# Batch 2's x groups one and a half units apart in a fused attention and bilinear-FFN kernel, and the loads of batches 4 to 7 issued one output later

## The chip, the cores and the metric

The kernel runs on one core of a Trainium2 chip. The metric is device time in microseconds (us) of one execution. The profile names the engines PE (TensorE matmul), PEld (TensorE weight load, which overlaps PE), DVE (VectorE), ACT (ScalarE), POOL (GpSimd) and SP (SyncE, here only a DMA issuer; its sequencer is SPq). L258 means line 258 of the kernel.

## The reference, cut to what matters

```python
# q, k, v: (8 batches, 8 heads, 576 tokens, 64)      w_a, w_b: (512, 1536)    w_out: (1536, 512)
kv  = einsum('bhsd,bhse->bhde', k, v)
out = einsum('bhsd,bhde->bhse', q, kv)                 # "x" before its normalization
x   = out / sqrt(mean(out**2, -1) + 1e-6) * g_norm     # heads joined: (4608 tokens, 512)
y   = ((x @ w_a) * (x @ w_b)) @ w_out                  # (4608, 512)
```

The FFN is most of the arithmetic. The attention is linear: one 64x64 matrix kv for each head, then q times kv, then a normalization over each head's 64 values.

## The kernel before

The 4608 tokens are cut into nine strips of 512. In strip s (counted from 0), PE makes 12 *units* (each 4 matmuls with w_a, then 4 with w_b, then ACT copies a out of PSUM and DVE multiplies b by it), and after them 4 *outputs* (12 matmuls with w_out each). In the strips 1 to 6 the attention of batch s+1 is made between those matmuls. Its places are counted in units and outputs: place 9 is behind unit 9, place 9.5 in the middle of unit 10, place 12 behind the first output, 15 behind the last.

A batch has 576 tokens, so five *chunks*: four of 128 tokens and one of 64. Each chunk passes through five steps on four engines.

```python
def tx(self, c, i):                       # x group of chunk c, into PSUM bank i
    t0 = c * 128
    n = min(128, S - t0)
    for p in range(NP):                   # 4 matmuls, 128 columns each
        nc.tensor.matmul(P[0:n, i, p * 128 : (p + 1) * 128],
                         lhsT=self.qT[:, p, t0 : t0 + n], rhs=kvb[self.b % 2][:, p, :],
                         start=True, stop=True)
    nc.scalar.activation(sqt[c % 3][0:n], P[0:n, i, :]..., AF.Square)
# tss(c): DVE sums the squares by head.   trs(c): ACT takes the reciprocal root, POOL multiplies
#         it by g into sqt[c % 3].
def txt(self, c, i):                      # the last reader of bank i
    nc.vector.tensor_mul(t[0:n], P[0:n, i, :]..., sqt[c % 3][0:n])
    nc.sync.dma_start_transpose(xt[:, :, t0 : t0 + n], ...)      # x, transposed, for the FFN
# ... cut ...
def slot(A, s, n):
    k0, xs = (5, (6.5, 7.5, 8.5, 9.5, 10.5)) if s == 1 else (2, (3.5, 5, 6, 7.5, 8.5))
    # ... the kv products at place k0: cut ...
    for c, x in enumerate(xs):
        i = 5 + c % 3                     # banks 5, 6, 7, then 5 and 6 again
        if n == x:          A.tx(c, i)
        elif n == x + 0.5:  A.tss(c)
        elif n == x + 1:    A.trs(c)
        elif n == x + 2.5:  A.txt(c, i)

for s in range(1, N_STRIP - 1):
    b = s + 1
    for n in range(FC + 4):               # 12 units, then 4 outputs
        # ... unit or output n, with slot(A, s, n - 0.5) in its middle: cut ...
        slot(A, s, n)
        if s == 1 and n == 3:
            load_late(3)
        if b + 1 < B and n == (12 if s == 1 else 8):
            transpose_q(b + 1)            # a DMA transpose on SP
        if b + 2 < B and n == 13:
            load_late(b + 2)              # POOL: waits for that transpose, then issues six DMAs
```

In these traces each engine works off its own instructions in the order in which the program names them; "The spacing alone" below shows what this costs when one of them waits (DVE stood for 9.77 us, at the end with two products ready behind it). Strip 1 starts its x groups later than the other strips (6.5 instead of 3.5), because batch 2's q, k and v are still on their way.

Of the kernel before, what the change touches and what calls it, by code (L numbers as in the profile page):

```python
# [15 lines left out]
def kernel(  # L16
# [13 lines left out]
    B, H, S, D = q.shape  # L30
# [102 lines left out]
    def load_late(b):  # L133
        if b > EARLY:

            nc.gpsimd.tensor_copy(gate, qT[(b - 1) % 2][0:1, 0, 0:1])
        d = qs_d[b].rearrange("t (h d) -> t h d", h=H)
        for hs in (slice(0, NP), slice(NP, H)):
            nc.gpsimd.dma_start(out=d[:, hs, :], in_=q[b, hs].rearrange("h t d -> t h d"))  # L139
        n = 128 * LC  # L140
        for t, src in ((ktl[b % 2], k), (vtl[b % 2], v)):
            nc.gpsimd.dma_start(
                out=t[:, :, 0:LC, :],
                in_=src[b, :, 0:n].rearrange("h (t c) d -> t h c d", c=LC),
            )
            nc.gpsimd.dma_start(
                out=t[0 : S - n, :, LC, :], in_=src[b, :, n:].rearrange("h t d -> t h d")
            )

    def transpose_q(b):  # L150
        nc.sync.dma_start_transpose(qT[b % 2], qs_d[b])
# [149 lines left out]
    class Unit:  # L301
        n = 0
# [36 lines left out]
    def ab_bank():  # L339
        n_ab[0] += 1  # L340
        return AB[(n_ab[0] - 1) % len(AB)]

    def ffn_ab(s, fc, between=None):
        u = Unit(s, fc, ab_bank(), ab_bank())
        u.part_a()
        if between:
            between()
        u.part_b()
# [38 lines left out]
    def ffn_o(s, g, i=O, between=None):  # L387
        o_mm(s, g, i, range(FC // 2))
        if between:
            between()  # L390
        o_mm(s, g, i, range(FC // 2, FC))
        o_out(s, g, i)
# [154 lines left out]
    def slot(A, s, n):  # L547

        kb = P[:, 7, 0 : NP * D].rearrange("q (p e) -> q p e", e=D)
        k0, xs = (5, (6.5, 7.5, 8.5, 9.5, 10.5)) if s == 1 else (2, (3.5, 5, 6, 7.5, 8.5))  # L550
        if n == k0:
            for p in range(NP):
                A.kv(p, kb[:, p, :])
            A.kv_out(slice(0, NP), kb)
        for c, x in enumerate(xs):
            i = 5 + c % 3
            if n == x:
                A.tx(c, i)
            elif n == x + 0.5:
                A.tss(c)  # L560
            elif n == x + 1:
                A.trs(c)
            elif n == x + 2.5:
                A.txt(c, i)

    for s in range(1, N_STRIP - 1):
        b = s + 1
        A = Attn(b) if b < B else None
        for n in range(FC + 4):
            amid = (lambda n=n: slot(A, s, n - 0.5)) if A else None  # L570
            if n >= FC:
                ffn_o(s, n - FC, ab_bank() if n % 2 else O, amid)
            elif s > 1 or n > 1:
                ffn_ab(s, n, amid)
            if A:
                slot(A, s, n)

            if s == 1 and n == 3:
                load_late(3)
            if b + 1 < B and n == (12 if s == 1 else 8):  # L580
                transpose_q(b + 1)
            if b + 2 < B and n == 13:
                load_late(b + 2)
    last = N_STRIP - 1
    for fc in range(FC):
# [41 lines left out]
```

## Time and profile before

| | before |
|---|---|
| median time, first 3 runs | 318.99 us |
| span in the profile | 317.4 us |
| PE busy | 310.9 us (98%) |
| strip 1, from its first unit to strip 2's | 34.65 us |
| each of strips 2 to 6 | 33.27 or 33.28 us |

PE is the engine that bounds the kernel. These are lines of the page of the kernel before: the span, and busy time, share of the span and number of instructions by engine.

```profile
span 317.4 us, 4979 instructions
...
PE 310.9 (98%) x1907; PEld 147.6 (46%) x1907; DVE 138.2 (44%) x230; ACT 115.8 (37%) x229; POOL 101.8 (32%) x124
```

A 98% busy PE hides what is lost, so the reading goes by stretches. This is the table of stretches of the kernel before, cut where the strips 1, 2 and 3 begin: start and end, length, then busy time of each engine, granted clock (PEclk, the share of its full clock that PE was given), DMA share and GB/s; the last two are not used here.

```profile
core 0: us, PE busy (x) PEld busy (x) DVE busy (x) ACT busy (x) POOL busy (x), PEclk, DMA share, GB/s
50.77:85.42 34.65, 33.48 (x205) 15.85 (x204) 16.46 (x26) 13.05 (x27) 11.76 (x12) 1.00 1.26 169
85.42:118.69 33.27, 33.27 (x205) 15.76 (x204) 15.71 (x24) 12.75 (x26) 18.49 (x19) 1.00 1.22 145
118.69:151.97 33.28, 33.28 (x206) 15.79 (x204) 15.70 (x24) 12.75 (x26) 11.86 (x12) 1.00 0.88 122
```

Strip 1 does the same matmuls in 1.37 us more. The list of PE's waits in the kernel before says where: who waited for whom, in total, how often, and the longest.

```profile
PE P L258 <- DVE qv L292: 1.2, 2, 0.6
```

The timeline of the kernel before shows the two places. First PE: start, length, what, and in brackets the idle time before it and what ended that. Between its x groups PE makes half a unit in 0.86 us (the printed 1.03 us contains the end of the last matmul, which overlaps the next).

```profile
68.53 1.03 PE L312 MATMUL P<-xt,wb_t 128*128 128x512 bf16 x4
69.40 1.03 PE L312 MATMUL P<-xt,wa_t 128*128 128x512 bf16 x4
71.01 0.38 PE L258 MATMUL P<-kvb,qT 128*128 128x128 bf16 x4 [0.58 <-DVE qv L292]
71.23 1.03 PE L312 MATMUL P<-xt,wb_t 128*128 128x512 bf16 x4
72.09 1.03 PE L312 MATMUL P<-xt,wa_t 128*128 128x512 bf16 x4
73.70 0.38 PE L258 MATMUL P<-kvb,qT 128*64 128x128 bf16 x4 [0.58 <-DVE qv L292]
```

Then DVE in the same kernel and stretch:

```profile
69.67 0.69 DVE L330 TENSOR_TENSOR ab<-P,asb 128x512 bf16<-128x512 f32 x1 [0.67 <-PE P L312]
70.28 0.68 DVE L292 TENSOR_TENSOR qv<-P,sqt 128x512 bf16<-128x512 f32 x1
```

The x group of chunk 3 is due at 69.40 + 0.86 = 70.26. Its bank, 5, still holds chunk 0. The last reader of chunk 0 is the DVE multiply L292, which stands behind unit 9's own product L330 and ends at 70.96. PE starts at 71.01, 0.75 us late; of this the profile shows 0.58 as idle, because it draws the last matmul to its modelled end. Chunk 4 repeats it one unit later. The Trainium skill ("Perfetto Trace Analysis", Optimization Strategy) says that the same gap repeating on the engine that should be saturated can mean that there is not enough SBUF or PSUM for the next tile; two equal gaps of 0.58 us before the only two x groups that reuse a bank are such a case.

### The profile page before, as it was taken

The numbers are of one execution on the slowest core, as the hardware profiler recorded it, in microseconds if no ns is written. First come the engines' busy times: TensorE is split into PE (matmuls) and PEld (weight loads), VectorE is DVE, ScalarE is ACT, GpSimd is POOL, SyncE is SP. The second block draws the span as 40 slices with busy tenths as digits, with TensorE's granted clock in tenths as the row PEclk, the third lists the DMA queues.
The fourth block names the chain that finished last, engine by engine and source line by source line (L and its number), as shares of the span: only waits on it lengthen the run. The fifth ranks groups of instructions, "written<-read, shape, count | busy, mean of one in ns | idle before, by whom it ended". The sixth has DMA issues, their size and how long they took to land.

```text
span 317.4 us, 4979 instructions
## 1 busy us (share of the span) xinstructions
PE 310.9 (98%) x1907; PEld 147.6 (46%) x1907; DVE 138.2 (44%) x230; ACT 115.8 (37%) x229; POOL 101.8 (32%) x124
## 2 busy tenths in 40 slices
PE   8999999999999999999999999999999999999995
PEld 3444454444445444544454445444544444444443
DVE  5543345367137613771258225741485144213421
ACT  3733155453246314640355025512461233123310
POOL 8944890193163550347023801310042000000000
PEclk9999999999999999999999999999999999999999
DMA  8999999999799799069916992363012300020002
GB/s 179 196 196 199 200 182 150 228 125 159 167 166 140 128 155 208 4 130 136 228 13 123 124 221 38 69 115 99 2 34 57 116 4 0 33 93 8 0 33 101
DMA packets 94237, 36.19 MB, mean 114 GB/s; under 512 B 64902, under 2 KB 89734, under 8 KB 94214
## 3 DMA queue, kind: packets, MB, share of 16 engines
q0 software_dynamic: 59120, 18.44, 53.4%
q1 hardware_dynamic: 34738, 17.01, 22.9%
q10 hardware_dynamic: 356, 0.43, 0.5%
q8 instruction: 15, 0.25, 0.3%
q14 instruction: 8, 0.07, 0.1%
HBM read 37.78 MB, written 12.98 MB: 160 GB/s over the span
## 4 chain that ended last, share of the span: by engine, by line
PE 85%; DMA 7%; POOL 4%; issue 1%; DVE 1%; ACT 0%; POOLq 0%; DVEq 0%
PE P L312 52%; PE P L369 28%; DMA wb_t<-in_moe_w_b_dram 6%; PE P L258 2%; PE P L168 2%; DMA vt<-in_v_dram 2%; POOL qt L116 1%; POOL wo_t L131 1%; POOL kt L116 1%; POOL vt L116 1%; POOL wa_t L427 0%; POOL wb_t L427 0%; DVE qv L292 0%; PE P L192 0%; PE P L219 0%
## 5 line engine op out<-in xcount | busy, mean ns | idle before, releaser
L330 DVE TENSOR_TENSOR ab<-P,asb 128x512 bf16<-128x512 f32 x108 | 74.5, 691 | 111.3 <-PE P L312 93.8
L312 PE MATMUL P<-xt,wa_t 128*128 128x512 bf16 x432 | 111.9, 379 | 0.0
L312 PE MATMUL P<-xt,wb_t 128*128 128x512 bf16 x432 | 111.7, 379 | 0.1
L326 ACT CAST asb<-P 128x512 bf16<-128x512 f32 x108 | 63.1, 586 | 91.2 <-PE P L312 91.2
L369 PE MATMUL P<-wo_t,ab 128*128 128x512 bf16 (+1 forms) x444 | 95.6, 373 | 0.0
L369 PEld LDWEIGHTS <-ab 128*128 128x128 bf16 x444 | 43.1, 98 | 49.1
L312 PEld LDWEIGHTS <-wa_t 128*128 128x128 bf16 x432 | 41.3, 98 | 47.1 <-issue 0.2
L312 PEld LDWEIGHTS <-wb_t 128*128 128x128 bf16 x432 | 41.2, 98 | 47.2 <-DMA wb_t<-in_moe_w_b_dram 0.6
L282 POOL TENSOR_TENSOR sqt<-rst,g_all 128x512 f32<-128x512 f32 (+1 forms) x24 | 25.0, 1044 | 97.4 <-ACT rst L275 97.4
L382 ACT COPY osb<-P 128x512 f32<-128x512 f32 x17 | 10.0, 586 | 74.2 <-PE P L369 59.6
L384 DVE COPY osb<-P 128x512 f32<-128x512 f32 x18 | 12.4, 691 | 47.2 <-PE P L369 42.6
L139 POOL DMA_DIRECT2D qs<-in_q_dram x12 | 19.8, 1655 | 1.2 <-issue 0.9
L271 DVE TENSOR_REDUCE sst<-sqt 128x8 f32<-128x512 f32 (+1 forms) x24 | 16.2, 676 | 0.8 <-ACT sqt L265 0.8
L292 DVE TENSOR_TENSOR qv<-P,sqt 128x512 bf16<-128x512 f32 (+1 forms) x24 | 16.2, 678 | 0.0
L265 ACT ACTIVATE sqt<-P 128x512 f32<-128x512 f32 (+1 forms) x24 | 14.2, 593 | 1.6 <-PE P L258 1.6
L258 PEld LDWEIGHTS <-qT 128*128 128x128 bf16 (+1 forms) x120 | 8.9, 100 | 9.5 <-issue 4.0
L258 PE MATMUL P<-kvb,qT 128*128 128x128 bf16 (+1 forms) x120 | 11.7, 220 | 1.2 <-DVE qv L292 1.2
L275 ACT ACTIVATE rst<-sst,eps_t 128x8 f32<-128x8 f32 (+1 forms) x30 | 9.0, 301 | 4.3 <-DVE sst L271 4.3
L179 ACT CAST kvb<-P 64x256 bf16<-64x256 f32 (+1 forms) x20 | 6.0, 301 | 11.3 <-PE P L168 11.2
L233 DVE SCALAR_TENSOR_TENSOR xt<-P,g_col,rs 128x288 bf16<-128x288 f32 x16 | 7.5, 512 | 5.2 <-ACT rs L223 5.2
L131 POOL DMA_DIRECT2D wo_t<-in_moe_w_out_dram x12 | 6.4, 533 | 6.7 <-DMA wb_t<-in_moe_w_b_dram 3.2
L282 POOL TENSOR_TENSOR k_x<-rst,g_all 128x512 f32<-128x512 f32 x6 | 6.3, 1044 | 7.0 <-ACT rst L275 7.0
(66 smaller groups left out, 120.4 us busy)
## 6 DMA issues: line engine op xcount, KB each, us to landing
out_dram<-osb SPq DMA_DIRECT2D x23, 256.0 KB, 2.4
qs<-in_q_dram POOLq DMA_DIRECT2D x12, 288.0 KB, 6.9
ktl<-in_k_dram POOLq DMA_DIRECT2D x6, 512.0 KB, 10.1
vtl<-in_v_dram POOLq DMA_DIRECT2D x6, 512.0 KB, 12.5
out_dram<-osb SPq DMA_DIRECT2D x13, 128.0 KB, 2.3
wo_t<-in_moe_w_out_dram POOLq DMA_DIRECT2D x12, 128.0 KB, 5.9
wa_t<-in_moe_w_a_dram POOLq DMA_DIRECT2D x5, 256.0 KB, 9.3
wb_t<-in_moe_w_b_dram POOLq DMA_DIRECT2D x5, 256.0 KB, 9.9
```

The lines of the kernel that those rows point to most:

```text
L139: nc.gpsimd.dma_start(out=d[:, hs, :], in_=q[b, hs].rearrange("h t d -> t h d"))
L258: nc.tensor.matmul(P[0:n, i, p * 128 : (p + 1) * 128], lhsT=self.qT[:, p, t0 : t0 + n], rhs=kvb[self.b % 2][:, p, :], start=True, stop=True,)
L265: nc.scalar.activation(sqt[c % 3][0:n], P[0:n, i, :].rearrange("t (h d) -> t h d", h=H), AF.Square)
L271: nc.vector.reduce_sum(sst[c % 3][0:n], sqt[c % 3][0:n], axis=mybir.AxisListType.X)
L282: nc.gpsimd.tensor_mul(sqt[c % 3][0:n], rst[c % 3][0:n].unsqueeze(2).to_broadcast([n, H, D]), g_all[0:n].unsqueeze(1).to_broadcast([n, H, D]),
L292: nc.vector.tensor_mul(t[0:n], P[0:n, i, :].rearrange("t (h d) -> t h d", h=H), sqt[c % 3][0:n])
L312: nc.tensor.matmul(self.a if w is wa_t else self.b, lhsT=w[:, kc, self.fc * 128 : (self.fc + 1) * 128], rhs=xt[:, kc, t0 : t0 + STRIP], st ...
L326: nc.scalar.copy(self.t, self.a)
L330: nc.vector.tensor_mul(abt[self.s % 2][self.fc], self.b, self.t)
L369: nc.tensor.matmul(P[:, i, e0:e1], lhsT=abt[s % 2][fc][:, g * 128 : (g + 1) * 128], rhs=wo_t[:, fc, e0:e1], start=(fc == 0), stop=(fc == F ...
L382: nc.scalar.copy(t, P[:, i, :])
L384: nc.vector.tensor_copy(t, P[:, i, :])
```

## The change

The intent is to keep the reuse of a bank away from its last reader, by spreading batch 2's x groups. Their steps then reach into the outputs, so the load that follows on POOL is moved behind the last of them.

```diff
-        k0, xs = (5, (6.5, 7.5, 8.5, 9.5, 10.5)) if s == 1 else (2, (3.5, 5, 6, 7.5, 8.5))
+        k0, xs = (5, (6.5, 8, 9.5, 11, 12.5)) if s == 1 else (2, (3.5, 5, 6, 7.5, 8.5))
...
-            if b + 2 < B and n == 13:
+            if b + 2 < B and n == 14:
                 load_late(b + 2)
```

Chunk 3 now comes at place 11, two units after chunk 0's multiply at place 9; before it was half a unit (9.5 against 9). The second edit holds for the loads of batches 4 to 7 alike. No operation is added or taken away.

## The prediction

> **What bounds the kernel now.** TensorE. The page gives PE 310.9 us busy of a 317.4 us span (98%), granted clock 0.999; the chain that ended last is 85% PE. The Trainium skill ("Trainium Kernel Development and Optimization", Performance Expectations) warns that matmul busy time is a poor measure because matmuls are pipelined, so I read stretches and idle times instead. The table of stretches, cut where each strip's first unit begins, gives 33.27 or 33.28 us for each of strips 2 to 6, and 34.65 us for strip 1 (50.77 to 85.42), with the same 204 to 206 matmuls. Strip 1, which holds batch 2's x, is 1.37 us too long. PE's waits name the cause: "P L258 <- DVE qv L292", 2 times, 1.2 us. In the timeline the fourth x group starts at 71.01 instead of 70.26 and the fifth at 73.70 instead of 72.95.
>
> **Why it waits.** Chunks rotate over PSUM banks 5, 6, 7. Chunk 3 reuses chunk 0's bank at place 9.5, half a unit (0.86 us of PE) after chunk 0's last reader, the DVE multiply, is issued at place 9. The multiply stands behind the unit's own product on DVE: product 69.67 to 70.28, multiply 70.28 to 70.96, so PE restarts at 71.01. Chunk 4 on chunk 1's bank repeats this. In later strips the same reuse is 1.5 units apart and no wait shows.
>
> **What the change does.** No work is added or removed. x groups go to 6.5, 8, 9.5, 11, 12.5. Chunk 3 now comes 2 units (3.4 us) after chunk 0's multiply is issued; product and multiply need 1.3 us. Chunk 4 likewise. Both waits should vanish whole. The last x group moves into the output groups (halves of 1.29 us of PE), where ACT and DVE idle 3 to 5 us before each eviction, so nothing should queue.
>
> The load of batch 4: GpSimd's built order is unchanged. At place 13 the load would stand in front of chunk 4's GpSimd multiply, now at 13.5; place 14 keeps it behind. Its first instruction waits for the transpose of batch 3's q (landed 85.62), not for the place, so it starts within 2 us of before. In later strips place 14 should do nothing.
>
> **The new risk.** Chunk 2's multiply is issued at place 12 instead of 11, behind the first output eviction; its DMA transpose moves behind that eviction's stores, from 76.48 to an estimated 78.1 us. Transposes here landed 3.5 to 7.2 us after issue, the slow ones while batch 3's load (last landing 78.2) was moving. I estimate a landing at 81.5 to 83; strip 2's first product needs it at about 84.2. Slack is 1 to 2.7 us: most likely nothing is lost.
>
> **Sum.** 1.37 us saved, all on the critical path, as PE runs without a gap from there to the last output. 318.99 - 1.37 = 317.6 us, 0.4% faster. Range 317.2 to 318.5. Chances: faster by over 2% 0.01, within 2% 0.98, slower 0.01.
>
> **What would show it.** Right: PE's wait for DVE qv is gone; strip 1's stretch is 33.3 us; PE busy is unchanged; strip 2 starts near 84.1. Wrong: PE idle at strip 2's first unit, released by a DMA of xt; or output matmuls waiting for DVE or ACT copies at 76 to 84 us; or batch 3's first GpSimd multiply (96.94) delayed by the load, and PE waiting in strip 2.
>
> **What would make it wrong.** Chunk 2's transpose landing over 6 us after its issue, slowed by the stores or q's transpose, eats the gain.

## The result, and the profile after

| | before | after |
|---|---|---|
| median, 6 runs each | 319.09 us (318.94 to 319.32) | 317.71 us (317.46 to 317.88) |
| span in the profile | 317.4 us | 316.0 us |
| PE busy | 310.9 us | 309.6 us |
| strip 1 | 34.65 us | 33.28 us |

The ratio is 0.9955, with a 95% interval of 0.9943 to 0.9968. A ratio here is the mean time of one kernel's fast runs over that of the other's fast runs of the same rounds, so it is not quite the ratio of the medians.

From the page of the changed kernel:

```profile
span 316.0 us, 4979 instructions
...
PE 309.6 (98%) x1907; PEld 147.0 (47%) x1907; DVE 138.5 (44%) x230; ACT 115.9 (37%) x229; POOL 101.7 (32%) x124
```

PE's busy time is 1.3 us less although its matmuls are the same. Only 0.20 us of this is in strip 1 (33.48 and 33.28 in the tables of stretches). By the same tables 1.05 us lies before strip 1 (48.83 and 47.78), in a stretch that is equally long in both kernels, so it has nothing to do with the gain.

The table of stretches of the changed kernel, cut at the same places of the program:

```profile
50.74:84.02 33.28, 33.28 (x206) 15.76 (x204) 16.65 (x26) 13.18 (x27) 11.93 (x13) 1.00 1.33 174
84.02:117.30 33.28, 33.28 (x206) 15.78 (x204) 15.70 (x24) 12.74 (x26) 18.31 (x18) 1.00 1.32 145
```

Strip 1 is now as long as every other; the strips 2 to 6 stay at 33.27 or 33.28 us, so the load's move does nothing in them. The list of PE's waits no longer has L258; all that it has is in the first 14 us. The timeline of PE in the changed kernel around the same two x groups:

```profile
71.97 1.03 PE L312 MATMUL P<-xt,wb_t 128*128 128x512 bf16 x4
72.83 0.39 PE L258 MATMUL P<-kvb,qT 128*128 128x128 bf16 x4
73.05 4.05 PE L369 MATMUL P<-wo_t,ab 128*128 128x512 bf16 x18
77.03 0.41 PE L258 MATMUL P<-kvb,qT 128*64 128x128 bf16 x4
77.37 6.65 PE L369 MATMUL P<-wo_t,ab 128*128 128x512 bf16 x30
83.86 1.03 PE L312 MATMUL P<-xt,wa_t 128*128 128x512 bf16 x4
```

There is no bracket with an idle time, at the x groups or at strip 2's first unit. Chunk 0's multiply ran on DVE from 70.03 to 70.71, two microseconds before chunk 3 wanted its bank at 72.83.

What the change postponed can be seen on SP. This is the timeline of SP in the changed kernel:

```profile
76.56 1.12 SPq L362 DMA_DIRECT2D out_dram<-osb  x2
77.77 1.24 SPq L296 DMA_TRANSPOSE xt<-qv  x1
79.18 2.38 SPq L151 DMA_TRANSPOSE qT<-qs  x1
```

Chunk 2's transpose is issued at 77.77 behind two stores (before: 76.48). The transpose of batch 3's q follows at 79.18 (before: 81.03), because chunk 3's transpose no longer stands in front of it. POOL's load waits for the landing of that transpose, so its first issue came at 84.07 instead of 85.92: written one output later, it started 1.85 us earlier.

### The profile page after: what moved, and what is told of

It is laid out like the page before. It is cut to its first block, busy times and chain, and to the rows that moved or that the text cites. A ratio compares the mean times of both kernels' runs of the same rounds, so it can differ in the third digit from the quotient of the medians.

```text
span 316.0 us, 4979 instructions
## 1 busy us (share of the span) xinstructions
PE 309.6 (98%) x1907; PEld 147.0 (47%) x1907; DVE 138.5 (44%) x230; ACT 115.9 (37%) x229; POOL 101.7 (32%) x124
## 4 chain that ended last, share of the span: by engine, by line
PE 95%; DMA 4%; issue 0%; POOL 0%; ACT 0%; POOLq 0%
PE P L312 59%; PE P L369 30%; PE P L258 2%; DMA qt<-in_q_dram 2%; DMA vt<-in_v_dram 2%; PE P L168 2%; PE P L219 0%; PE P L192 0%; PE P L245 0%; PE P L206 0%; ACT o_end L595 0%; POOL ident masks.py:199 0%; POOL ident masks.py:197 0%; POOLq masks.py:199 0%; POOLq L611 0%
## 5 line engine op out<-in xcount | busy, mean ns | idle before, releaser
L312 PE MATMUL P<-xt,wa_t 128*128 128x512 bf16 x432 | 111.9, 379 | 0.0
L312 PE MATMUL P<-xt,wb_t 128*128 128x512 bf16 x432 | 111.8, 379 | 0.0
L312 PEld LDWEIGHTS <-wb_t 128*128 128x128 bf16 x432 | 41.3, 98 | 47.7 <-DMA wb_t<-in_moe_w_b_dram 0.6
L312 PEld LDWEIGHTS <-wa_t 128*128 128x128 bf16 x432 | 41.1, 98 | 47.0 <-issue 0.2
L292 DVE TENSOR_TENSOR qv<-P,sqt 128x512 bf16<-128x512 f32 (+1 forms) x24 | 16.3, 678 | 0.0
L258 PEld LDWEIGHTS <-qT 128*128 128x128 bf16 (+1 forms) x120 | 8.9, 100 | 8.2 <-issue 2.5
L258 PE MATMUL P<-kvb,qT 128*128 128x128 bf16 (+1 forms) x120 | 11.7, 220 | 0.0
```

The costliest lines, as they stand in the source:

```text
L258: nc.tensor.matmul(P[0:n, i, p * 128 : (p + 1) * 128], lhsT=self.qT[:, p, t0 : t0 + n], rhs=kvb[self.b % 2][:, p, :], start=True, stop=True,)
L292: nc.vector.tensor_mul(t[0:n], P[0:n, i, :].rearrange("t (h d) -> t h d", h=H), sqt[c % 3][0:n])
L312: nc.tensor.matmul(self.a if w is wa_t else self.b, lhsT=w[:, kc, self.fc * 128 : (self.fc + 1) * 128], rhs=xt[:, kc, t0 : t0 + STRIP], st ...
```

## The experiments

My theory was: PE waited for one thing only, the PSUM bank whose last reader is the DVE multiply. The distance in the program between that multiply and the reuse is what counts, and the load's move costs nothing and gains nothing by itself, but keeps POOL's order right. The rivals were: the load's earlier start gave part of the gain; five chunks one unit apart crowd DVE, ACT or POOL; the three scratch buffers in SBUF, which rotate like the banks, hold the chain up. Eight kernels were run, all with correct results. The time before was 319.06 us in the first four's rounds and 319.14 us in the others' (9 runs each).

### The load alone

```diff
 (kernel before)
-            if b + 2 < B and n == 13:
+            if b + 2 < B and n == 14:
```

> The kernel before with only the load moved from place 13 to 14. My theory: nothing else of GpSimd stands between the two places in any strip, and its first instruction waits for the transpose of q, so the built order of GpSimd is the same and the time stays at 319.1 us, with both PE waits of about 0.6 us. Rival (part of the gain came from the load, which started 1.85 us earlier after the change): 0.3 us or more faster.

Measured: 319.02 us (5 runs), ratio 0.9997, interval 0.9984 to 1.0011. PE's waits are those of before:

```profile
PE P L258 <- DVE qv L292: 1.2, 2, 0.6
```

The load's place by itself is worth nothing. What made the load start earlier in the changed kernel was the spacing, which moved the transpose of q forward on SP. That earlier start can't be part of the gain either: in the kernel before, strip 2, which runs beside this load, is already as short as the other strips (33.27 us).

### The spacing alone

```diff
 (changed kernel)
-            if b + 2 < B and n == 14:
+            if b + 2 < B and n == 13:
```

> The changed kernel with the load of batch 4 left at place 13. My theory: the two PE waits stay away, but the load now stands on GpSimd in front of chunk 4's multiply (place 13.5). Its first instruction waits for the transpose of batch 3's q (landed 83.8 us in the changed kernel) and its issues take 6.5 us, so the multiply ends near 91.6 us; the DVE multiply behind it holds up strip 2's first product on DVE, and PE stops near 88.3 us for about 4.5 us. Expected 322.2 us, with an idle time of PE of 4 to 5 us in strip 2. Rival (the load's place does not matter, the spacing is the whole change): 317.7 us, no wait in strip 2.

Measured: 325.08 us (4 runs), ratio 1.0184, interval 1.017 to 1.0198. So with the spacing alone the kernel is 1.8% *slower* than before. The chain of events is the expected one. POOL, then DVE, then PE in this kernel's timeline:

```profile
83.96 0.18 POOL L136 COPY gate<-qT 1x1 bf16<-1x1 bf16 x1 [7.78 <-DMA qT<-qs]
...
90.90 1.10 POOL L282 TENSOR_TENSOR sqt<-rst,g_all 64x512 f32<-64x512 f32 x1
```

```profile
92.03 0.68 DVE L292 TENSOR_TENSOR qv<-P,sqt 64x512 bf16<-64x512 f32 x1 [9.77 <-POOL sqt L282]
92.64 1.27 DVE L330 TENSOR_TENSOR ab<-P,asb 128x512 bf16<-128x512 f32 x2
```

```profile
87.41 1.03 PE L312 MATMUL P<-xt,wa_t 128*128 128x512 bf16 x4
93.36 1.87 PE L312 MATMUL P<-xt,wb_t 128*128 128x512 bf16 x4 [4.93 <-DVE ab L330]
```

The load stands in front of chunk 4's POOL multiply and waits for the transpose of q; the multiply ends at 92.0 (91.6 was expected). On DVE the multiply L292 waits for it with 9.77 us of idle time, and the products of strip 2's first two units, whose matmuls had ended by 87.6, wait behind it. The Trainium skill ("PSUM — Partial Sum Buffer", section Engine vs sequencer instructions) calls the queues of ScalarE, VectorE and GpSimd strict FIFO; this is what it looks like. PE then lacks a free bank and stands for 4.93 us, where 4 to 5 was expected.

The time was expected at 322.2 and is 2.9 us more. The expectation left out the clock. Four matmuls that take 1.03 us take 1.87 us after the stop, and the table of stretches of this kernel shows the granted clock:

```profile
88.00:93.00 5.00, 0.44 (x3) 0.10 (x1) 0.97 (x2) 0.59 (x1) 4.00 (x5) 0.83 2.04 188
93.00:95.00 2.00, 1.64 (x4) 0.41 (x3) 0.91 (x2) 0.00 (x0) 0.00 (x0) 0.50 1.45 197
```

The trace's clock records put the half clock at 91.26 to 98.09. PE worked in it from 93.36 on, for 4.73 us, and so lost about half of that, 2.37 us. Estimated from these: 317.71 + 4.93 + 2.37 = 325.0, which meets the measured 325.08. All four runs show a mean clock of 0.989. The Trainium skill ("TensorE: Matmul & The Clock Gate", What's actually happening) describes a half-rate state after at least one idle window of about 3.4 us. That it came after a stop of 4.93 us agrees; but it began 2.83 us after PE stopped (88.43 to 91.26), before so long an idle time had passed.

### The reuse one unit after the reader

```diff
 (kernel before)
-        k0, xs = (5, (6.5, 7.5, 8.5, 9.5, 10.5)) if s == 1 else ...
+        k0, xs = (5, (6.5, 7.5, 8.5, 10, 11)) if s == 1 else ...
```

> The kernel before with only chunks 3 and 4 moved half a unit later (10 and 11), so that a bank is reused 1 unit after the place of its last reader instead of half a unit; chunks 0 to 2 stay one unit apart. My theory (PE waits only for the bank): product and multiply on DVE need 1.3 us plus a start of about 0.25 us, less than the 1.73 us of a unit, so both waits vanish: 317.7 us. Rival (the chunks stand too close together for DVE and ACT, so that one and a half units between all of them are needed): a part of the waits stays, 318.2 us or more.

Measured: 317.68 us (5 runs), ratio 0.9954, interval 0.9942 to 0.9967, and no wait of L258. Half a unit for two chunks, with the load left where it was, has the whole gain of the change. The chunks 0 to 2 are still one unit apart, so crowding is not the cause. The last step on POOL is at place 12 here, so the load at 13 is harmless.

### The reuse directly at the reader

```diff
 (kernel before)
-        k0, xs = (5, (6.5, 7.5, 8.5, 9.5, 10.5)) if s == 1 else ...
+        k0, xs = (5, (6.5, 7.5, 8.5, 9, 10)) if s == 1 else ...
```

> The kernel before with chunks 3 and 4 moved half a unit earlier (9 and 10), so that a bank is reused directly at the place of its last reader. My theory: each wait grows by the half unit of PE work (0.86 us) that no longer stands between, from 0.75 to 1.6 us, so 320.8 us, and PE's idle times before the two x groups are 1.4 to 1.6 us each. Rival (the waits have another cause, such as GpSimd held by the load of batch 3 until 68.8 us): the end of the wait does not follow the place, and the time stays within 0.5 us of 319.1.

Measured: 320.79 us (5 runs), ratio 1.0057, interval 1.0044 to 1.007. PE's waits:

```profile
PE P L258 <- DVE qv L292: 2.9, 2, 1.4
```

The loss moved with the distance: two idle times of 1.45 us at no distance, 0.58 us at half a unit, none at one unit. The difference, 0.87 us, is the half unit of matmuls (0.86 us) that no longer fills the time.

### Another bank for chunk 3

```diff
 (kernel before)
-            i = 5 + c % 3
+            i = O if s == 1 and c == 3 else 5 + c % 3                            # O is bank 3
...
-                ffn_o(s, n - FC, ab_bank() if n % 2 else O, amid)
+                ffn_o(s, n - FC, ab_bank() if n % 2 or s == 1 else O, amid)
```

> The kernel before, all places unchanged, but chunk 3 of batch 2 goes to PSUM bank 3, which is free until the output groups (these rotate over the other banks in strip 1). My theory (the wait is for the bank): the first of the two waits vanishes and the second stays, 318.4 us, one PE idle time of about 0.6 us before the fifth x group. Rival (the places themselves crowd DVE, ACT or GpSimd): both waits stay, 319.1 us.

Measured: 318.32 us (5 runs), ratio 0.9976, interval 0.9963 to 0.9988. One wait is gone and one stays:

```profile
PE P L258 <- DVE qv L292: 0.6, 1, 0.6
```

No place was moved here: chunk 3 stands at place 9.5 as before and its bank is another. (To keep bank 3 free for it, the outputs of strip 1 rotate over the other banks; chunk 4's wait of 0.59 us shows that this alone takes no wait away.) This is the most direct proof that the wait is for the bank.

### More scratch, same banks

```diff
 (kernel before)
+    for t in rs[0:2]:      # two buffers that are free by then, so sqt has five
+        sqt.append(t.rearrange("p a b -> p (a b)")[:, 0 : H * D].rearrange("p (h d) -> p h d", h=H))
-    sst, rst: range(3)                     sqt[c % 3], sst[c % 3], rst[c % 3]
+    sst, rst: range(5)                     sqt[c % 5], sst[c % 5], rst[c % 5]
```

> The kernel before, places and PSUM banks unchanged, but five scratch buffers for the squares, sums and reciprocal roots of the chunks instead of three, so that no chunk waits for another's scratch. My theory (the wait is for the PSUM bank alone): no change, 319.1 us, both PE waits stay. Rival (the reuse of the scratch in SBUF holds up the chain): the waits shrink, 318.4 us or less.

Measured: 319.13 us (5 runs), ratio 1.0, interval 0.9986 to 1.0014, both waits as before (1.2 us, 2 times). The scratch buffers rotate with the same period as the banks and could be suspected as well; they are not the cause.

### Chunk 2 two units later

```diff
 (changed kernel)
-        k0, xs = (5, (6.5, 8, 9.5, 11, 12.5)) if s == 1 else ...
+        k0, xs = (5, (6.5, 8, 11.5, 12, 12.5)) if s == 1 else ...
```

> The changed kernel with chunk 2 two units later (11.5; chunks 3 and 4 at 12 and 12.5), so that its multiply stands at place 14 behind the third output eviction. A measure of the slack that I estimated at 1 to 2.7 us. My theory: the multiply ends near 82.7 us, its DMA transpose is issued behind two stores near 83.2 us and lands 3.3 to 4.3 us later, at 86.5 to 87.5 us, while PE would begin strip 2 at 84.0: an idle time of 2.5 to 3.5 us at strip 2's first unit, released by the DMA of xt, 320.7 us. Rival (strip 2 does not need the chunk so soon, or the transposes land faster): 317.7 us, no idle time there.

Measured: 319.80 us median of 4 runs (319.59 to 319.87, and the profiled one 322.04), ratio to before 1.0038, interval 1.001 to 1.0066. PE's waits in the profiled run:

```profile
PE P L312 <- DMA xt<-qv: 2.9, 1, 2.9
```

The new risk that the prediction named is real, and this run measures how far away it was. Chunk 2's multiply began at 81.93 instead of 76.45, 5.48 us later; its transpose was issued at 82.93 and landed at 86.67, and PE stood for 2.93 us. If the landing took as long in the changed kernel, its slack was 5.48 - 2.93 = 2.55 us (an estimate from these numbers; the changed kernel's trace does not record that landing). The prediction had 1 to 2.7 us. The other three runs give more: they took 2.0 us longer than the changed kernel (319.74 - 317.71), so the slack was about 3.5 us in them, if PE's stop is all that was lost (also an estimate).

The idle time is as expected; the median is 0.9 us under the expected 320.7, while the profiled run is above it. In that run the clock records show half clock from 86.21 to 89.62, which began 2.33 us after PE stopped. Two stretches of its table, before and in the half clock:

```profile
83.88:86.20 2.32, 0.00 (x0) 0.00 (x0) 0.00 (x0) 0.58 (x1) 2.32 (x3) 1.00 0.98 104
86.20:89.70 3.50, 2.89 (x8) 1.03 (x9) 0.00 (x0) 0.58 (x1) 2.85 (x4) 0.51 1.93 167
```

PE worked in half clock from 86.81 to 89.62 and so lost half of 2.81 us; estimated from these, 317.71 + 2.93 + 1.40 = 322.04, which is what was measured. The other three runs have a mean clock of at least 0.999, and their times (319.59 to 319.87) are below the 320.64 us that a stop of 2.93 us alone would give, so they must have stood less, about 2.0 us. One of four runs paid the clock on top. I have no trace of the other three, and why PE stood longer in one is not shown.

### The last chunk with 128 weight columns

The profile pointed at one more loss, in every strip: the last x group, of 64 tokens, takes 0.34 us of the chain of waits where the others take 0.22. Here 128 tokens are multiplied (64 of them a second time), and the steps after it use partitions 64 to 127.

```diff
 (changed kernel)
-            t0 = c * 128
-            n = min(128, S - t0)
+            t0 = min(c * 128, S - 128)
+            r = slice(c * 128 - t0, 128)        # the rows that are new
             for p in range(NP):
-                    P[0:n, i, ...], lhsT=self.qT[:, p, t0 : t0 + n], ...
+                    P[:, i, ...],   lhsT=self.qT[:, p, t0 : t0 + 128], ...
 (tss, trs, txt and the square: rows 0:n become r)
```

> The changed kernel, and the last x chunk of each batch, 64 tokens, is multiplied as 128 rows (the 64 rows before it are computed again and not used; the results stand on partitions 64 to 127). The last x group takes 0.34 us of the chain where the others take 0.22. My theory (PE pays for the change from 64 weight columns to 128 and back): the six last groups shrink to 0.22 us each, 0.7 us in all, 317.0 us. Rival (the 0.12 us has another cause): 317.7 us. If the theory holds this beats both kernels.

Measured: 316.33 us (316.04 to 316.69, 4 runs), ratio to before 0.9914, interval 0.99 to 0.9927. It beats both kernels, and the gain over the changed kernel is 317.71 - 316.33 = 1.38 us, twice what was expected. The table of stretches of this kernel, strips 1 and 2:

```profile
50.58:83.64 33.06, 32.85 (x202) 15.83 (x204) 16.85 (x26) 13.29 (x27) 11.76 (x12) 1.00 1.33 173
83.64:116.69 33.05, 32.89 (x202) 15.82 (x204) 15.91 (x24) 13.01 (x26) 18.48 (x19) 1.00 1.29 150
```

A strip is 0.22 or 0.23 us shorter, and six of them make 1.3 to 1.4 us. (The missing matmuls in the count, x202, are records that this trace lost.) The chain of waits shows where, at the last x group of strip 2 and the 20 matmuls after it: start, length, what. First the changed kernel, then this one (its source is two lines longer, so L312 is L314 here):

```profile
102.18 0.34 PE P L258 x4
102.52 4.42 PE P L312 x20
```

```profile
101.79 0.22 PE P L258 x4
102.02 4.32 PE P L314 x20
```

The timeline of the weight loads shows why. First the changed kernel, at the same group:

```profile
100.94 0.75 PEld L312 LDWEIGHTS <-wa_t 128*128 128x128 bf16 x4
102.10 0.25 PEld L258 LDWEIGHTS <-qT 128*64 128x64 bf16 x4 [0.42 <-issue]
102.45 0.55 PEld L312 LDWEIGHTS <-wb_t 128*128 128x128 bf16 x4
```

Then this kernel, at the same place:

```profile
101.41 0.43 PEld L258 LDWEIGHTS <-qT 128*128 128x128 bf16 x4
101.80 0.59 PEld L314 LDWEIGHTS <-wb_t 128*128 128x128 bf16 x4
```

With 128 columns the first weight load starts while the matmul before it still streams: at 101.41, when its own matmul starts at 101.63. With 64 columns it starts at 102.10, together with its matmul at 102.11. The same happens on the way back to 128 columns, at 102.45. A change of the number of weight columns thus costs about 0.1 us each way in this stream, and I had counted only the one that shows in the x group itself; the other one sat in the group after it (4.42 against 4.32 us). The Trainium skill ("TensorE: Matmul & The Clock Gate", Step-by-step: what each phase is for) says that PE pulls weight loads ahead of matmuls in flight when the row groups do not conflict or the load goes to the background buffer; that section has no word of a change of columns.

The same trace has the case elsewhere. The kv products of the strips 1 to 6 (L168) load 64 columns too. In the changed kernel, strip 2, first PEld, then PE:

```profile
89.13 0.71 PEld L168 LDWEIGHTS <-ktl 128*64 128x64 bf16 x40 [0.42 <-issue]
89.88 0.55 PEld L312 LDWEIGHTS <-wa_t 128*128 128x128 bf16 x4
89.13 0.82 PE L168 MATMUL P<-vtl,ktl 128*64 128x64 bf16 x40
```

The first load starts with its matmul here as well, and so does the first load of 128 columns after it (89.88, its matmul at 89.89). From 39 us on, this holds at each of the 32 changes between 128 and 64 columns that can be paired in this trace: the load is at most 0.005 us ahead. Where the number of columns stays, the first load of a group is at least 0.04 us ahead, and 0.21 us behind matmuls of 512 columns. So it is not peculiar to the x groups: it goes with a change of the number of columns. Whether the cause is the column count as such, or what the compiler encodes for it, no run here tells.

## Why the prediction was right

- **The time.** Predicted 317.6 us in 317.2 to 318.5; measured 317.71. Predicted saving 1.37 us; measured 319.09 - 317.71 = 1.38.
- **The cause.** The prediction said that PE waits for the bank because its last reader stands half a unit in front. The distance runs (1.45, 0.58 and 0 us of idle time), the other bank (one wait gone) and the scratch (nothing) show this, and rule out the rivals that I could name.
- **The size.** It was taken from the surplus of strip 1 over the other strips (34.65 - 33.28), not from the idle times of the profile (1.2 us), which leave out the part of the wait that is drawn as the end of a matmul. Strip 1 came out at 33.28. (Twice the 0.75 us of lateness would be 1.50, too much: about 0.1 us of the second start's lateness is the change to 64 weight columns, which a strip without a wait pays too. In the changed kernel the last group of strip 2 starts 0.96 us after the half unit before it, at 102.11 after 101.15, where the other groups start after 0.86.)
- **The critical path.** PE runs without a gap from strip 1 to the last output, so the time saved there arrived whole at the end.
- **The load of batch 4.** Right that its place in itself does nothing (319.02 us), and that its start is set by the transpose of q: it came 1.85 us earlier. Right also that at place 13 it would stand in front of chunk 4's multiply; the prediction did not put a number on that, and it is the largest effect: 325.08 us.
- **The new risk.** Chunk 2's transpose was estimated to be issued at 78.1 and was at 77.77; the slack of 1 to 2.7 us was 2.55 by the later run's trace, but about 3.5 us by its three runs without one (both estimates). That nothing was lost is measured; the size of the slack is confirmed only in part.
- **A by-point that missed.** PE's busy time was said to stay unchanged, and fell by 1.3 us, 1.05 us of it before strip 1, where the two kernels are the same and take the same time. It was no good witness.

Two expectations of experiments were short, both by a term left out: the clock after a long stop of PE (2.4 us), and the second change of weight columns (0.1 us in each strip). A third, for chunk 2 two units later, was 0.9 us too long at the median.

## What to carry to other kernels

When a saturated engine has small equal gaps, compare a stretch that should repeat with its neighbours, and find what the gap waits for; here half a unit of distance between a bank's last reader and its reuse was worth 0.4%, and one unit was enough. When work is moved later, look in the built order at what it comes to stand behind on every in-order engine: the spacing without the load's move lost 1.8%, because one load on POOL held a DVE multiply, and that held the next strip's products. A stop of PE can cost more than its length: here the half clock added 2.4 us to a stop of 4.93 us, and 1.4 us to one of 2.93 us. A short tail chunk can cost less when it is padded to the full width (here 1.38 us less over six batches).

## What the Trainium skill lacked or had wrong

- "TensorE: Matmul & The Clock Gate" (What's actually happening) gives half clock after at least one idle window of about 3.4 us. Here it came 2.33 us after PE stopped, in a stop of 2.93 us, in one run of four; in a stop of 4.93 us it came 2.83 us after PE stopped, and all four runs have the same mean clock of 0.989. The half-clock stretches lasted 3.41 and 6.83 us, one and two of the page's windows of 3413 ns, which agrees with it. The page does not say that a single stop shorter than a window can trigger it.
- The same page (Step-by-step: what each phase is for) lacks the case of weight loads that are not pulled ahead: between loads of 128 and of 64 columns the load started together with its matmul (102.10 and 102.11 us) instead of 0.22 us ahead, about 0.1 us for each change and 0.22 us in each strip.
- No page that I read has the time that a small DMA transpose takes to land under load: 7.2 us for the first chunk while batch 3's load was moving, 3.5 us for the last chunk, issued 6.4 us after that load had landed (the kernel before, 70.98 and 84.65 us). The last chunk has half as many tokens, so the two do not separate the load's part from the size's.
